# k_m and v_m as plain f32 products with the k and v tiles stationary

## The chip, the core and the metric

The kernel runs on one core of a Trainium2 chip. A core has TensorE (PE, matrix products; PEld is its weight load), VectorE (DVE), ScalarE (ACT) and GpSimd (POOL), and DMA queues, of which SyncE's (SP) carries most loads here. A matrix product takes a *stationary* operand, loaded as weights, and streams a *moving* operand past it; results go to one of eight PSUM banks. The metric is the device time of one execution in microseconds (us); the median of three runs before the change is 1393.74 us.

## The reference

Eight batches, eight heads, 576 rows of length 64, 32 memory slots; then a dense mixture of four experts over all 4608 rows.

```python
a = exp(phi - phi.max(axis=2)); a = a / (a.sum(axis=2) + 1e-9)     # over the 576 rows
k_m = einsum('bhsm,bhsd->bhmd', a, k)
v_m = einsum('bhsm,bhsd->bhmd', a, v)
scores = (q @ k_m^T) / 8
attn = exp(scores - scores.max(-1)); attn = attn / (attn.sum(-1) + 1e-9)
x = (attn @ v_m) laid out as 4608 x 512
p = domain_probs / (domain_probs.sum(-1) + 1e-9)
out = sum over e of p[:, e] * (relu(x @ w1[e]) @ w2[e])             # 512 -> 1024 -> 512
```

All arrays are f32, and the result has to be good to more digits than one rounded product gives.

## The kernel before

**Precision.** TensorE takes f32 in two ways here. The big products run on `float32r` tiles, a rounded form. Where more digits are needed a tile is split in two float32r parts: ACT casts it (the high part) and POOL or DVE subtracts the cast from the original (the low part). A product of split operands is three float32r products (high·high, high·low, low·high). Transposes (a product with the identity `ident`) and `scores_mm` (q·k_m) run on plain f32 tiles, not split.

**Stages.** Batches are worked in four pairs; each pair is 128 *steps* (`PAIR`), four experts of 32. Attention never forms `attn @ v_m`: the kernel multiplies v_m by w1 (`vw_mm`, `vw_out`, tiles `vw`, or `four_*` and DRAM for later experts), and a step's `first(s)` multiplies that by the transposed softmax `AT` (L641 to L643), applies relu (ACT L653, DVE L655) to make `h`, and `second(s)` multiplies `h` by `w2` (L674 to L676) into an accumulating bank. The last two pairs use another scheme with fewer products (`unit`, L916 to L918 and L1002).

**k_m and v_m, the part that changes.** For each batch `phi` is exponentiated and normalized (`phi_max`, `phi_exp`, `phi_norm`), turned by transposes (`phi_turn`, `phi_turn_tail`) and split into tile `a` (L308/L309, L323/L324): 128 rows of s by (high, low) by two heads by 32 slots. k and v of a head pair `hp` come as one 512 KB load, `kv`, four chunks of 128 rows with k beside v, into one of four `stage` buffers; `kv_split` casts and subtracts it (L345, L346) into `kvs`. `kv_mm` (L357) then takes `a` (high and low side by side, 128 columns) as weights and streams the 256 columns of k and v: for each chunk one product with the high part of kv and one with the low part. The last 64 rows come as `kvt`, loaded twice over so that high and low sit on different halves of the partitions (`tail_split`, L331/L332), and are one product (`kv_mm_tail`, L360). The sum has slots in rows; `kv_out` copies it (L368), `kv_fold` transposes it back (L377, `ident`), and `kv_pick` copies the high half and adds the low half into `kT` and `v` (L394, L396).

**Order.** `at(s, unit)` puts units in a plan by step; the tables `UNITS_1`, `ATT` and so on set them by hand. From step 36 on, and in the start-up before step 0, instructions stand in the order of the program; for steps 0 to 35 a scheduler orders them. Batch 0's k_m and v_m are made in the start-up, batch 1's in the scheduled steps, batches 2 to 7 at hand-set steps beside the expert products. Loads into `stage` are issued in plan order, three takes ahead (`take`, `stage_ahead`). The four banks "pm" are shared by `first`, `vw_mm`, the transposes and the k_m/v_m sums in rotation. `keep_warm` issues idle products of `ident`.

**Softmax over slots.** `soft` sums each row's 32 exponentials (L490), adds 1e-9 (L491), takes the reciprocal (L492) and multiplies (L493).

Of the kernel before, what the change touches and what calls it, by code (L numbers as in the profile page):

```python
# [61 lines left out]
UNITS_1 = (1, 5, 5, 6, 5, 6, 8, 9, 10, 11, 11, 12, 17, 13, 13, 20)  # L62
# [21 lines left out]
def body(ctx: ExitStack, tc: tile.TileContext, qm, qt, kv, kvt, phi, prob, w1, w1d, w2, out):  # L84
# [41 lines left out]
    def stage_ahead(upto):  # L126
        while count[0] < min(upto, len(order)):
# [16 lines left out]
            )  # L144
            nc.sync.dma_start(t, src)
# [131 lines left out]
    def phi_norm(b, g):  # L277
# [27 lines left out]
    def phi_turn_out(b, g):  # L305
        src = st["tpa", b, g].rearrange("p c a m -> p a c m")
        dst = st["a", b][:, 2 * g:2 * g + 2, :4]
        nc.scalar.copy(dst[:, :, :, 0, :], src)  # L308
        nc.vector.tensor_sub(dst[:, :, :, 1, :], src, dst[:, :, :, 0, :].bitcast(F32))  # L309
        give(st["tpa", b, g])  # L310

    def phi_turn_tail(b):
        ph = st["ph", b]
        tp = bank("pm", NP, 2 * M)
        for g in range(2):
            nc.tensor.transpose(
                tp[:, 2 * g:2 * g + 2].rearrange("p a m -> p (a m)"), ph[:, g, 512:], ident
# [3 lines left out]
    def phi_turn_tail_out(b):  # L321
        a, tp = st["a", b], st["tpb", b]
        nc.scalar.copy(a[:, :, 4, 0, :], tp)  # L323
        nc.vector.tensor_sub(a[:, :, 4, 1, :], tp, a[:, :, 4, 0, :].bitcast(F32))  # L324
# [9 lines left out]
    def unit_tail(b):
        def emit(raw):
            for h in range(2):
                tail_split(b, raw, h, nc.gpsimd)
        return ("kvt", b), emit

    def kv_split(b, hp, raw, c2, eng):  # L340
        tag = {"tag": "kvs", "bufs": KVS} if b else {"tag": "vw1", "bufs": 5}
        t = att.tile([P, 2, 512], F32R, name="kvs", **tag)
        t = t.rearrange("p s (i d) -> p s i d", i=2)
        src = raw[:, 2 * c2:2 * c2 + 2].rearrange("p c w d -> p c (w d)")
        nc.scalar.copy(t[:, 0], src)  # L345
        eng.tensor_sub(t[:, 1], src, t[:, 0].bitcast(F32))  # L346
        st["kvs", b, hp, c2] = t

    def kv_mm(b, hp, c2):
        if c2 == 0:  # L350
            st["x", b, hp] = bank("pm", 2 * P)
        x, a, t = st["x", b, hp], st["a", b], st["kvs", b, hp, c2]
        for i in range(2):
            c = 2 * c2 + i
            lhs = a[:, hp, c].rearrange("p s m -> p (s m)")
            for s in range(2):
                nc.tensor.matmul(x, lhs, t[:, s, i, :], start=c + s == 0, stop=False)  # L357

    def kv_mm_tail(b, hp):
        nc.tensor.matmul(  # L360
            st["x", b, hp],
            st["a", b][:, hp, 4].rearrange("p s m -> p (s m)"), st["tail", b][:, hp, :],
            start=False, stop=True,
        )

    def kv_out(b, hp):
        xs = att.tile([P, 2 * P], F32, name="xs", tag="xs", bufs=2)
        nc.scalar.copy(xs, st["x", b, hp])  # L368
        give(st["x", b, hp])
        st["xs", b, hp] = xs  # L370
# [903 lines left out]
```

## Time and profile before

| | |
|---|---|
| median of 3 runs | 1393.74 us (1391.53 to 1394.98) |
| profiled execution | 1392.14 us, span of its instructions 1390.3 us |
| TensorE busy | 1362.0 us, 98% of the span |
| DVE, ACT, POOL busy | 841.3, 625.4, 617.4 us (61%, 45%, 44%) |
| granted TensorE clock, mean | 0.997 |
| DMA | 301.37 MB, 217 GB/s |

A row of the profile names the line, engine and operation, the tiles written and read, the shape and the count. "128\*128 128x256" on a PE row is the weights (rows\*columns) and then the output. Durations of PE rows overlap, since products are pipelined: what a product costs in a stream is the distance from its start to the next start, which I take from merged timeline rows (first column start, second length, both us; "x8" is eight records merged).

### The profile page before, as it was taken

The page shows a single profiled execution, that of the slowest core. Times are in us where ns is not written, and L with a number is a line of the kernel's source. Part 1 is how long each engine was busy: PE and PEld are TensorE (multiplying, and loading weights), DVE is VectorE, ACT ScalarE, POOL GpSimd, SP SyncE. Part 2 cuts the span into 40 slices and gives each one's busy share as a digit, 9 for nine tenths or more (in the row PEclk, how much of TensorE's full clock was granted, in tenths as well). Part 3 has the DMA queues.
Part 4 walks back from the last instruction along what each step waited for, and adds up shares of the span by engine and source line. Part 5 has one row for each costly group of instructions (what it writes and reads, how often), then busy time and mean ns, then how long its engine had stood idle before and what let it go on. Part 6 is the DMA issues. An engine that isn't in the chain of part 4 may idle for free.

```text
span 1390.3 us, 25223 instructions
## 1 busy us (share of the span) xinstructions
PE 1362.0 (98%) x8894; PEld 1248.4 (90%) x8894; DVE 841.3 (61%) x1894; ACT 625.4 (45%) x1536; POOL 617.4 (44%) x652
## 2 busy tenths in 40 slices
PE   7999999999999999999999999999999999999998
PEld 6788888788888888889888998999999999999998
DVE  7875535446755365454434467777767666666666
ACT  6765555443345465463344354555543333333332
POOL 4400354745353424433144375677753334443432
PEclk9999999999999999999999999999999999999999
DMA  6742354897675364354598898899984866666661
GB/s 255 240 165 76 117 182 173 311 322 240 210 281 212 107 229 146 125 203 143 178 290 296 277 321 292 286 344 311 326 298 131 259 186 177 180 173 175 175 181 75
DMA packets 102029, 301.37 MB, mean 217 GB/s; under 512 B 24976, under 2 KB 26128, under 8 KB 101904
## 3 DMA queue, kind: packets, MB, share of 16 engines
q1 hardware_dynamic: 81168, 224.26, 51.9%
q0 software_dynamic: 19584, 71.31, 13.0%
q10 hardware_dynamic: 1152, 4.19, 0.7%
q8 instruction: 71, 1.16, 0.3%
q14 instruction: 54, 0.44, 0.1%
HBM read 213.46 MB, written 84.93 MB: 215 GB/s over the span
## 4 chain that ended last, share of the span: by engine, by line
PE 89%; DVE 4%; DMA 2%; issue 2%; ACT 1%; SPq 0%; POOL 0%; DVEq 0%; ACTq 0%; POOLq 0%
PE banks L1002 22%; PE banks L676 9%; PE banks L674 9%; PE banks L675 9%; PE banks L916 5%; PE banks L917 5%; PE banks L918 5%; PE banks L641 5%; PE banks L642 4%; PE banks L643 4%; PE banks L579 3%; PE banks L463 2%; PE banks L357 2%; DMA stage<-in_w 1%; PE banks L1040 1%
## 5 line engine op out<-in xcount | busy, mean ns | idle before, releaser
L1020 DVE SCALAR_TENSOR_TENSOR acc<-banks,pt,acc 128x256 f32<-128x256 f32 x416 | 200.0, 481 | 107.7 <-PE banks L1002 104.2
L160 POOL TENSOR_TENSOR w<-stage,w 128x512 fp32r<-128x512 f32 x134 | 177.0, 1332 | 188.7 <-ACT w L159 179.4
L655 DVE SCALAR_TENSOR_TENSOR h<-banks,h 128x256 fp32r<-128x256 f32 x256 | 107.3, 420 | 168.6 <-ACT h L653 111.4
L676 PE MATMUL banks<-w,h 128*128 128x512 f32 x512 | 201.2, 393 | 3.4 <-DVE h L655 3.4
L674 PE MATMUL banks<-w,h 128*128 128x512 f32 x512 | 201.9, 394 | 0.1
L675 PE MATMUL banks<-w,h 128*128 128x512 f32 x512 | 201.4, 393 | 0.0
L653 ACT ACTIVATE h<-banks 128x256 fp32r<-128x256 f32 x256 | 98.0, 384 | 199.8 <-PE banks L643 169.9
L641 PE MATMUL banks<-AT,vw 128*128 128x256 f32 (+1 forms) x512 | 156.6, 306 | 3.7 <-DVE h L655 1.8
L1002 PE MATMUL banks<-w,a 128*128 128x256 f32 x1080 | 154.4, 282 | 0.3 <-DVE acc L1020 0.2
L643 PE MATMUL banks<-AT,vw 128*128 128x256 f32 (+1 forms) x512 | 150.9, 295 | 1.2 <-DVE vw L556 1.2
L916 PE MATMUL banks<-AT,vw 128*128 128x256 f32 (+1 forms) x512 | 151.6, 296 | 0.0
L642 PE MATMUL banks<-AT,vw 128*128 128x256 f32 (+1 forms) x512 | 151.3, 296 | 0.0
L917 PE MATMUL banks<-AT,vw 128*128 128x256 f32 (+1 forms) x512 | 151.1, 295 | 0.0
L918 PE MATMUL banks<-AT,vw 128*128 128x256 f32 (+1 forms) x512 | 150.9, 295 | 0.0
L1002 PEld LDWEIGHTS banks<-w,a 128*128 128x128 f32 x1080 | 143.6, 188 | 4.8 <-issue 0.9
L983 POOL TENSOR_TENSOR vt<-ph,vt 128x512 fp32r<-128x512 f32 x64 | 84.1, 1314 | 107.3 <-ACT vt L982 78.3
L676 PEld LDWEIGHTS banks<-w,h 128*128 128x128 f32 x512 | 96.3, 188 | 25.8 <-DVE h L655 4.3
L346 POOL TENSOR_TENSOR kvs<-stage,kvs 128x512 fp32r<-128x512 f32 x58 | 75.4, 1317 | 93.2 <-ACT kvs L345 87.3
L641 PEld LDWEIGHTS banks<-AT,vw 128*128 128x128 f32 x512 | 96.8, 189 | 13.8 <-DVE vw L556 3.8
L674 PEld LDWEIGHTS banks<-w,h 128*128 128x128 f32 x512 | 96.4, 188 | 12.0 <-ACT h L653 0.4
L675 PEld LDWEIGHTS banks<-w,h 128*128 128x128 f32 x512 | 96.4, 188 | 10.9
L159 ACT CAST w<-stage 128x512 fp32r<-128x512 f32 x168 | 102.7, 619 | 4.5 <-DMA stage<-in_w 2.1
(149 smaller groups left out, 2985.4 us busy)
## 6 DMA issues: line engine op xcount, KB each, us to landing
w<-kw SPq DMA_DIRECT2D x93, 512.0 KB, 5.5
vwd<-vst POOLq DMA_DIRECT2D x80, 512.0 KB, 6.4
vw<-vwd SPq DMA_DIRECT2D x320, 128.0 KB, 6.0
w<-v SPq DMA_DIRECT2D x55, 512.0 KB, 5.6
stage<-in_w SPq DMA_DIRECT2D x44, 512.0 KB, 4.5
stage<-in_w1d SPq DMA_DIRECT2D x40, 512.0 KB, 5.3
stage<-in_kv SPq DMA_DIRECT2D x32, 512.0 KB, 4.3
kw<-w POOLq DMA_DIRECT2D x24, 512.0 KB, 5.6
```

Source lines behind the costliest of these rows:

```text
L160: eng.tensor_sub(dst[:, 1, :], raw, dst[:, 0, :].bitcast(F32))
L641: nc.tensor.matmul(ps, w[:, 0, f], at_t[:, g, 0, c], start=g == 0, stop=False)
L642: nc.tensor.matmul(ps, w[:, 0, f], at_t[:, g, 1, c], start=False, stop=False)
L643: nc.tensor.matmul(ps, w[:, 1, f], at_t[:, g, 0, c], start=False, stop=g == 1)
L674: nc.tensor.matmul(po[t], x[:, 0, :], w[:, 0, :], start=j == 0, stop=False)
L675: nc.tensor.matmul(po[t], x[:, 0, :], w[:, 1, :], start=False, stop=False)
L676: nc.tensor.matmul(po[t], x[:, 1, :], w[:, 0, :], start=False, stop=j == NJ - 1)
L916: nc.tensor.matmul(ps, w[:, 0, f], at_t[:, g, 0, c], start=g == 0, stop=False)
L917: nc.tensor.matmul(ps, w[:, 0, f], at_t[:, g, 1, c], start=False, stop=False)
L918: nc.tensor.matmul(ps, w[:, 1, f], at_t[:, g, 0, c], start=False, stop=g == 1)
L1002: nc.tensor.matmul(ps, a[:, l, jj], w[:, r, c], start=start and jj + i == 0, stop=jj == 1 and i == 2, skip_group_check=True,)
L1020: VE.scalar_tensor_tensor(a, src, p, a, ALU.mult, ALU.add)
```

## The change

Five things:

1. `a` and the tail `tl` become plain f32, not split; `kv_split`, `tail_split`, `kv_out`, `kv_fold` are gone. `kv_mm` takes the raw `stage` tile as weights (128 rows by the 128 columns of k or v of a head pair) and streams `a` of that pair (64 columns), so that the result has the 64 entries of k or v in rows, as `kT` and `v` want it. Per batch: 4 pairs, k and v, 4 chunks and a tail, that is 40 products.
2. All of a batch's sums lie in one bank (`kvp`), picked by four copies.
3. `kvt` is loaded once over (64 rows, 256 KB), straight into `tl` by `load_tail`, outside the `stage` rotation.
4. The start-up's order is rewritten; for batch 0 the low half of `vt` is subtracted by POOL, not by DVE.
5. In `soft` the addition of 1e-9 becomes a sum over a pair whose second element is 1e-9 from a memset.

The hand-set steps: batches 2 to 7 multiply at s+13, s+14, s+15, s+16 (one pair a step) and pick at s+17; before, they multiplied at s+12, s+15, s+18, s+21. The tail's step in `UNITS_1` goes from 5 to 2.

```diff
     def phi_turn_out(b, g):
         src = st["tpa", b, g].rearrange("p c a m -> p a c m")
-        dst = st["a", b][:, 2 * g:2 * g + 2, :4]
-        nc.scalar.copy(dst[:, :, :, 0, :], src)
-        nc.vector.tensor_sub(dst[:, :, :, 1, :], src, dst[:, :, :, 0, :].bitcast(F32))
+        (nc.vector.tensor_copy if b == 0 and g else nc.scalar.copy)(
+            st["a", b][:, 2 * g:2 * g + 2, :4], src
+        )
...
+    def load_tail(b):
+        st["tail", b] = att.tile([P, NP, 2 * P], F32, name="tl", tag="tl")
+        nc.sync.dma_start(st["tail", b][:64], kvt[b])
+
+    def kv_mm(b, hp, raw):
+        if hp == 0:
+            st["kvp", b] = bank("pm", 2, NP, 2 * M)
         for w in range(2):
+            x = st["kvp", b][:, w, hp]
+            for c in range(4):
+                nc.tensor.matmul(x, raw[:, c, w], st["a", b][:, hp, c], start=c == 0, stop=False)
+            nc.tensor.matmul(
+                x, st["tail", b][:64, hp, P * w:P * w + P], st["a", b][:64, hp, 4],
+                start=False, stop=True,
             )
...
     def soft(b, t0):
...
-        nc.vector.reduce_sum(zv[:, :, 0], av, AX.X)
-        nc.vector.tensor_scalar_add(zv[:, :, 0], zv[:, :, 0], 1e-9)
+        sums_z = guarded.popleft()
+        guarded.append(sums_z)
+        nc.vector.reduce_sum(sums_z[:n, :nt * H, 0], av, AX.X)
+        nc.vector.reduce_sum(zv[:, :, 0], sums_z[:n, :nt * H], AX.X)
...
-        at(s + 9, unit_tail(b))
+        at(s + 6, lambda: load_tail(b))
         for hp in range(NP):
...
-            at(s + 10 + 3 * hp, (("kv", b, hp), load))
-            at(s + 12 + 3 * hp, multiply)
-            at(s + 13 + 3 * hp, lambda hp=hp: kv_out(b, hp))
-        for g in range(2):
-            at(s + 18 + 6 * g, lambda g=g: [kv_fold(b, 2 * g + i) for i in range(2)])
-            at(s + 19 + 6 * g, lambda g=g: kv_pick(b, g))
+            at(s + 13 + hp, (("kv", b, hp), lambda raw, hp=hp: kv_mm(b, hp, raw)))
+        at(s + 13 + NP, lambda: kv_pick(b))
```

The new line numbers: `kv_mm` L339 and L340 (tail), transposes L303 and L319, `scores_mm` L415, `vw_mm` L489 to L491, `first` L595 to L597, `second` L628 to L630, `keep_warm` L1060, splits L163/L164.

On PE, in the start-up, where batch 0's sums end and the first scores begin (`kvs`, `tl`, `a` as above, `xs` the copied sum, `w` a split w1 tile, `vt` the split v_m). Before:

```order
L360 MATMUL banks<-tl,a 128x256
L377 MATMUL banks<-ident,xs 128x128 x4
L357 MATMUL banks<-kvs,a 128x256 x8
L360 MATMUL banks<-tl,a 128x256
L1118 MATMUL banks<-ident 128x128 x3
L463 MATMUL banks<-kT_78,stage 128x64 x4
L377 MATMUL banks<-ident,xs 128x128 x4
L1118 MATMUL banks<-ident 128x128 x5
L463 MATMUL banks<-kT_78,stage 128x64 x4
L1118 MATMUL banks<-ident 128x128 x2
L535 MATMUL banks<-w_255,vt_82 128x512
```

After:

```order
L339 MATMUL banks<-a,stage 128x64 x4
L340 MATMUL banks<-a,stage 128x64
L415 MATMUL banks<-kT_78,stage 128x64 x8
L1060 MATMUL banks<-ident 128x128 x4
L489 MATMUL banks<-w_242,vt_82 128x512
```

The transposes between the halves of the scores are gone; the scores follow the last sum directly.

On POOL, in the start-up, behind the memsets. Before:

```order
L115 MEMSET vt_83 128x1024
L346 TENSOR_TENSOR kvs<-stage,kvs 128x512
L332 TENSOR_TENSOR tl<-stage,tl 64x512
L346 TENSOR_TENSOR kvs<-stage,kvs 128x512
L332 TENSOR_TENSOR tl<-stage,tl 64x512
L160 TENSOR_TENSOR w_255<-stage,w_255 128x512
```

After:

```order
L115 MEMSET vt_83 128x1024
L118 MEMSET zg_90 128x16
L118 MEMSET zg_91 128x16
L378 TENSOR_TENSOR vt_82<-v,vt_82 64x2x32 x4
L164 TENSOR_TENSOR w_242<-stage,w_242 128x512
L164 TENSOR_TENSOR w_245<-stage,w_245 128x512
L164 TENSOR_TENSOR vh<-v,vh 128x128
```

POOL's splits of k, v and the tail are gone; four subtractions for `vt` now stand ahead of the w1 splits.

On PE, for batch 2, one head pair at its step. Before:

```order
L676 MATMUL banks<-w_1375,h 128x512
L357 MATMUL banks<-kvs,a 128x256 x8
L360 MATMUL banks<-tl,a 128x256
L377 MATMUL banks<-ident,xs 128x128 x4
L641 MATMUL banks<-AT,vw 128x320
```

After:

```order
L630 MATMUL banks<-w_1112,h 128x512
L339 MATMUL banks<-a,stage 128x64 x4
L340 MATMUL banks<-a,tl 128x64
L339 MATMUL banks<-a,stage 128x64 x4
L340 MATMUL banks<-a,tl 128x64
L595 MATMUL banks<-AT,vw 128x256
```

Nine products of 256 columns and their transposes become ten products of 64 columns, read from the loaded `stage` tile itself.

More of the change, by code (lines that the diff above doesn't have):

```diff
@@ L60 @@
 }
[L62 removed]
+UNITS_1 = (1, 5, 5, 6, 2, 6, 8, 9, 10, 11, 11, 12, 17, 13, 13, 20)
 W1_1 = (10, 10, 12, 13)
@@ L115, in body @@
         nc.gpsimd.memset(t, 0.0)
+    guarded = deque(const.tile([P, 2 * H, 2], F32, name=f"zg{i}") for i in range(2))
+    for t in guarded:
+        nc.gpsimd.memset(t[:, :, 1], 1e-9)
     pt = const.tile([P, N // P, E], F32, name="pt")
@@ L144, in stage_ahead @@
             )
+            t = t[:src.shape[0]]
             nc.sync.dma_start(t, src)
@@ L334, in unit_tail @@
[L334 to L370, printed above, removed]
-    def kv_fold(b, hp):
-        g = hp // 2
-        if hp % 2 == 0:
-            st["kvp", b, g] = bank("pm", 2, 2, P)
-        for w in range(2):
-            nc.tensor.transpose(
-                st["kvp", b, g][:, hp % 2, w, :], st["xs", b, hp][:, w * P:(w + 1) * P], ident
-            )
-    def kv_pick(b, g):
-        if g == 0:
+    def load_tail(b):
+        st["tail", b] = att.tile([P, NP, 2 * P], F32, name="tl", tag="tl")
+        nc.sync.dma_start(st["tail", b][:64], kvt[b])
@@ L387, in kv_pick @@
                 r, m = slice(64 * i, 64 * i + 64), slice(M * i, M * i + M)
[L388 to L397 removed]
+                dst = st["v", b][r, hps] if w else kT[b % 4][r, hps, m]
+                (nc.vector.tensor_copy if b == 0 and i else nc.scalar.copy)(
+                    dst, st["kvp", b][r, w, hps, m]
+                )
+        if hps.stop == NP:
+            give(st["kvp", b])
     def unit_kv(b, hp):
         def emit(raw):
[L401 to L410 removed]
+            kv_mm(b, hp, raw)
+            if hp == NP - 1:
+                kv_pick(b)
         return ("kv", b, hp), emit
@@ L1150, in body @@
-        kv_split(0, 3, kvr(3), 0, dve)
+        st["tail", 0] = raw["kvt", 0]
+        q = raw["qm", 0, 0]
         for hp in range(2):
-            for c2 in range(2):
-                kv_mm(0, hp, c2)
-            kv_mm_tail(0, hp)
-        kv_split(0, 3, kvr(3), 1, dve)
-        for hp in range(2):
-            kv_out(0, hp)
-        for hp in (2, 3):
-            for c2 in range(2):
-                kv_mm(0, hp, c2)
-            kv_mm_tail(0, hp)
-            if hp == 2:
-                for i in range(2):
-                    kv_fold(0, i)
@@ L1177, in body @@
-        kv_pick(0, 1)
+        kv_pick(0, slice(2, 4))
         scores_mm(0, 0, q, (2, 3))
         scores_max(0, 0)
-        split_w1(w1g[0], 0, 1, gps)
-        write_vt_0(0, slice(1, 2))
-        keep_warm(2)
-        split_w1(w1g[1], 0, 2, gps)
-        split_w1(w1g[1], 0, 3, gps)
-        pv = [vw_mm(0, 0, hp, ("p2", 4)) for hp in range(4)]
+        write_vt_0(0, gps)
+        keep_warm(4)
+        w1g = [raw["w1", 0, 0, g] for g in range(2)]
+        for hp in range(2):
+            split_w1(w1g[0], 0, hp, gps)
@@ L1186, in body @@
         scores_exp(0, 0)
-        vw_out(pv[0], 0, 0, 0, 0, (0,))
+        pv = [vw_mm(0, 0, hp, ("p2", 4)) for hp in range(2)]
+        for hp in range(2, 4):
+            split_w1(w1g[1], 0, hp, gps)
+        pv += [vw_mm(0, 0, hp, ("p2", 4)) for hp in range(2, 4)]
         soft(0, 0)
-        keep_warm(3)
-        for hp in (1, 2):
+        for hp in (0, 1):
             vw_out(pv[hp], 0, 0, 0, hp, (0,))
@@ L1194, in body @@
         transposes_out(0, 0)
-        vw_out(pv[3], 0, 0, 0, 3, (0,))
+        for hp in (2, 3):
+            vw_out(pv[hp], 0, 0, 0, hp, (0,))
         for i in range(2):
```

86 lines of the change are left out of this document (18 added, 68 removed).

## The prediction

> **What bounds the kernel now.** I read the busy times first, then TensorE's share by stretches, then its rows by shape and the distances between them, then its waits, last the start-up in order of time. The page and the stretches (length, then busy time and records of each engine, granted clock, DMA share, GB/s):
>
> ```profile
> PE 1362.0 (98%) x8894; PEld 1248.4 (90%) x8894; DVE 841.3 (61%) x1894; ACT 625.4 (45%) x1536; POOL 617.4 (44%) x652
> ...
> 0.00:40.00 40.00, 28.52 (x177) 24.98 (x178) 31.21 (x65) 26.15 (x61) 17.86 (x23) 0.96 0.69 252
> 40.00:60.00 20.00, 18.62 (x113) 15.73 (x112) 17.75 (x39) 16.03 (x35) 7.21 (x6) 1.00 0.69 234
> 60.00:780.00 720.00, 710.85 (x4006) 620.49 (x4005) 377.52 (x852) 339.82 (x888) 282.58 (x273) 1.00 0.60 203
> ```
>
> From 60 us on PE has a product in flight nearly always, and the other engines about half the time. There the time is the sum of PE's distances; work taken from DVE, ACT and POOL is worth only the PE waits that it causes. Before 60 us PE is idle 11.5 + 1.4 us, and DVE is the busiest. So the change has two prices: PE's own products (everywhere), and the start-up.
>
> **PE's price of k_m and v_m.** First the rows by shape (busy, mean ns):
>
> ```profile
> L357 PE MATMUL banks<-kvs,a 128*128 128x256 f32 x256 | 36.3, 284 | 2.8 <-DVE a L309 1.9 <-DVE kvs L346 0.9
> L463 PE MATMUL banks<-kT,stage 128*128 128x64 f32 x256 | 30.8, 272 | 0.8 <-DVE kT L396 0.7
> L377 PE MATMUL banks<-ident,xs 128*128 128x128 f32 x64 | 10.0, 273 | 0.0
> L360 PE MATMUL banks<-tl,a 128*128 128x256 f32 x32 | 9.1, 284 | 0.4 <-DVE a L324 0.4
> L463 PE MATMUL banks<-kT,stage 128*64 128x64 f32 x64 | 5.4, 228 | 0.3 <-DVE AT L526 0.3
> ```
>
> L463, q·k_m, is the nearest row to a new product: plain f32 on both sides, 128 rows, 128 columns of weights, 64 columns streamed. The count tells the main thing. The program has 8 batches of two 256-row groups with 8 such products, 128 in all; the profile has 256 records. L357 has 256 products and 256 records, L377 64 and 64. So a plain f32 product runs as two records, each with its own weight load, a float32r one as one. What a record takes is read from distances:
>
> ```profile
> 523.29 0.39 PE L676 MATMUL banks<-w,h 128*128 128x512 f32 x1
> 523.52 1.89 PE L463 MATMUL banks<-kT,stage 128*128 128x64 f32 x16
> 525.22 0.36 PE L641 MATMUL banks<-AT,vw 128*128 128x256 f32 x1
> ...
> 590.71 1.11 PE L357 MATMUL banks<-kvs,a 128*128 128x256 f32 x8
> 591.65 0.28 PE L360 MATMUL banks<-tl,a 128*128 128x256 f32 x1
> 591.77 0.60 PE L377 MATMUL banks<-ident,xs 128*128 128x128 f32 x4
> 592.12 0.36 PE L641 MATMUL banks<-AT,vw 128*128 128x256 f32 x1
> ...
> 38.29 0.68 PE L463 MATMUL banks<-kT,stage 128*64 128x64 f32 x8
> 38.90 0.50 PE L535 MATMUL banks<-w,vt 128*128 128x512 f32 x1
> ```
>
> - Old product: (591.65 - 590.71)/8 = 0.1175 us. Old fold: (592.12 - 591.77)/4 = 0.0875 us.
> - New product: (525.22 - 523.52)/16 = 0.106 us a record, 0.2125 us a product. With weights 64 columns wide the record takes (38.90 - 38.29)/8 = 0.076: the width of the weights matters though the stream is 64 columns both times. The new weights are 128 wide.
>
> A batch gave up 32 + 4 products and 8 folds, 36 x 0.1175 + 8 x 0.0875 = 4.93 us, and gets 40 x 0.2125 = 8.50. Net +3.57 us a batch. Batches 1 to 7 lie in the PE-bound stretch: **+25.0 us**. The tail's 8 products a batch have 64 rows of weights, which no plain f32 row shows. From below they are bounded by the 0.076 of the narrow row (112 records x 0.030 = 3.4 us less), from above by 0.106; I take 0.106, because the narrow row differs in columns, which the tail does not. The Trainium skill, "TensorE: Matmul & The Clock Gate", section LDWEIGHTS, says that a weight load takes its columns over 1.2 in ns whatever the rows, 107 ns for 128; by that the tail's price is the one taken, and no price here falls below it. The 128-wide rows agree (0.106 a record); for 64 columns it would be 53 ns and the trace has 76. The transposes of phi's tail get narrower weights (2 a batch): 14 x at most 0.03, nothing.
>
> **What the other engines give back.** Their splits go (POOL's L346 and L332, ACT's L345, L331, L368, DVE's L309, L324, L396). After 60 us only PE's waits count; the longest of them:
>
> ```profile
> PE banks L579 <- ACT h L653: 2.5, 1, 2.5
> PE banks L676 <- DVE h L655: 2.0, 1, 2.0
> PE banks L1002 <- DVE acc L1020: 1.9, 4, 1.2
> PE banks L641 <- DVE h L655: 1.8, 1, 1.8
> PE banks L641 <- DVE vw L556: 1.7, 3, 0.9
> ```
>
> The second is the pair sum's business. DVE and POOL at that place:
>
> ```profile
> 333.73 0.68 DVE L490 TENSOR_REDUCE z<-at 128x16 f32<-128x512 f32 x1
> 334.10 5.49 POOL L160 TENSOR_TENSOR w<-stage,w 128x512 fp32r<-128x512 f32 x4
> 334.44 5.19 DVE L491 TENSOR_SCALAR z<-z 128x16 f32<-128x16 f32 x1
> ...
> 339.67 0.25 DVE L492 RECIPROCAL z<-z 128x16 f32<-128x16 f32 x1
> ```
>
> Adding 1e-9 to 16 numbers took 5.19 us, until POOL's run of four subtractions ended; the sum beside it (L490) was not held. The `h` that stood behind it on DVE came late, and PE waited 2.0 us. The new sum is of L490's kind, so I count these 2.0 us as gained. Of the others, L579 waits behind `vst`'s transfers and L1002 behind the accumulation, neither touched; of the two L641 rows (3.5 us) ACT's lighter load may give back a little, 0 to 2. I take 2.5 in all, bounds 0 and 5.
>
> **The start-up.** Which instructions carry it now:
>
> ```profile
> 7.12 1.14 ACT L345 CAST kvs<-stage 128x512 fp32r<-128x512 f32 x2 [0.82 <-DMA stage<-in_kv]
> 7.98 0.38 PE L316 MATMUL banks<-ident,ph 128*128 128x128 f32 x2
> ...
> 20.91 1.10 PE L463 MATMUL banks<-kT,stage 128*128 128x64 f32 x8 [0.68 <-DVE kT L396]
> 26.24 0.39 PE L537 MATMUL banks<-w,vt 128*128 128x512 f32 x1
> 30.06 1.11 PE L514 MATMUL banks<-ident,at 128*128 128x128 f32 x4 [2.76 <-DVE at L493]
> 32.53 0.77 PE L641 MATMUL banks<-AT,vw 128*128 128x256 f32 x2
> 37.17 0.50 PE L676 MATMUL banks<-w,h 128*128 128x512 f32 x1 [1.37 <-DVE h L655]
> ...
> 17.79 1.27 POOL L160 TENSOR_TENSOR w<-stage,w 128x512 fp32r<-128x512 f32 x1 [3.52 <-ACT w L159]
> 28.39 0.46 POOL L160 TENSOR_TENSOR vh<-v,vh 128x128 fp32r<-128x128 f32 x1 [3.06 <-ACT vh L159]
> 32.42 1.66 ACT L159 CAST w<-stage 128x512 fp32r<-128x512 f32 x3
> ```
>
> The new chain: kv's first load is there at 7.1, the turns end near 8.4. 40 products take 8.5 us (to 16.9), 8 score products 1.7: the last score stands at 18.6, before at 20.91 + 0.9. The softmax is then ready about 4 us later (max, subtract, exp, sum and product, each of 512 elements a row as L490 above, 0.68, and two small ones). But PE's next work, the 12 v·w1 products, waits for POOL, and that chain is the later one: v is picked at 17.3, four `vt` subtractions of at most 0.46 end by 19.1, four w1 splits of 1.27 with `vh` 0.46 among them by 24.7. The last product ends at 25.4 (before 26.5), and the transposes, behind it on PE, start there, not at 30.06. From the transposes to the first `first` it is 2.5 us (30.06 to 32.53), through the same cast and subtraction: 27.9. From there to L676 it is 4.6 us, 1.4 of them PE's wait for an `h` that DVE made late behind splits; ACT still has casts ahead of the first relu (four, where the row above has three in 1.66), so I leave 3.2 us. The first complete `second` is at about 31, where L676 now starts at 37.17: **-6 us**, bounds -2 (POOL's chain stretched, and the 1.4 kept) and -9 (transposes bound by the softmax alone). From there to 60 us DVE is nearly full; it loses L309, L324 and POOL's company, worth at most the 1.4 us of PE idle in that stretch: -1. What `kvt`'s half load saves ahead of the products is within these bounds.
>
> **New waits.** PE now reads `stage` itself, so a late kv load stops PE, with all that is queued on it; before, it stopped ACT two steps ahead. One place is tight. The third kv load of batch 3 now stands behind the sixteen small copies of batch 2's v on SP's queue; the first and the last of them:
>
> ```profile
> 193.90 0.60 SPq L448 DMA_DIRECT2D vs<-vh  x1
> 206.69 0.61 SPq L450 DMA_DIRECT2D vt<-vh  x1
> ```
>
> They hold the queue 13.4 us. The product that needs the load comes three steps after the copies are due; a step is six products at 0.1175 and six at 0.23 (523.29 to 523.52), 2.1 us, and one with kv work 4.2, so about 10.5 us pass. 0 to 4 us may be lost; I take 0.5. `load_tail` is three steps ahead of its use on the same queue, and `tl` is free by then. One bank of "pm" is held five steps on end; three remain for `first`, which needs a bank again only three steps later: nothing.
>
> **The sum.** 25.0 - 2.5 - 6 - 1 + 0.5 = +16.0 us. The profiled execution took 1392.14 (span 1390.3), so 1408.1; the median of the runs is 1.6 above it, so **1409.5**.
>
> **Rivals.**
>
> 1. *A product costs what its 256 streamed columns cost in float32r (faster).* Then 280 products x 0.1175 = 32.9 against 34.5 given up, -1.6, and with -9.0 for the rest 1383. Against it stand the two records of every L463 product. It decides below (34.5 + 9.0 - 4.2)/280 = 0.140 us a product; 0.2125 was measured. The Trainium skill, "FP8 and Floating Point Precision", section TensorE Precision Notes, gives true f32 four passes through the array; four passes of 64 columns would be this rival, and the two records speak against that reading. Chance 0.03.
> 2. *The records run at the narrow row's pace (no change).* 560 x 0.076 = 42.6, +8.1, less 9.0: 1393. Against it: the 16 records in a row of L463 with just the new shape. Chance 0.05.
> 3. *PE starves for kv.* Each of batches 2 to 7 waits once for a load or a bank, 1 to 2 us, and batch 3 the full 4: +8 to +14 on top, 1418 to 1424. For it: the queue row above; against it: loads are three takes ahead, 11 us or more. Chance 0.12.
>
> My forecast has 0.80. A measurement of this kernel can tell about 0.3%, 4.2 us, from no change. Faster by more: 0.03 and a little, 0.04; within: 0.05; slower: 0.91. The forecast's own bounds: 25.0 less 3.4, gains of 12 to 4 in the start-up and the waits together, new waits 0 to 4: 1403 to 1418. For 8 in 10 I widen it to 1401 and, towards the third rival, 1420.
>
> **What the profile after would show.** L339 with 512 records and L340 with 128, sixteen of a kind at 0.106 us from start to start; else the PE term falls. The span from 60 us on longer by about 3.6 us for each batch, in the stretches where the kv products stand, and nowhere else. The first L630 near 31 us; the 1e-9 sum never above 0.3 us; the 2.0 us wait of `second` gone. A PE wait on `stage` at L339, above all in batch 3, would be the third rival.

## Result, and the profile after

The changed kernel takes 1434.89 us (median of 6 runs, 1433.82 to 1441.27) against 1394.11: 1.0306 times as long, 95% interval 1.0284 to 1.0328. The forecast was 1409.5 us, with a range of 1401 to 1420. The sign was right; the loss is 41 us instead of 16. The profiled execution has a span of 1432.8 us, 42.5 more than before's.

The page, busy times and the granted clock in 40 slices:

```profile
PE 1412.0 (99%) x9164; PEld 1290.2 (90%) x9164; DVE 799.0 (56%) x1793; ACT 566.8 (40%) x1375; POOL 524.7 (37%) x584
...
PEclk7999999999999999999999999999999999999999
```

The other engines lost work as the diff says, PE's share rose, and the first slice has a clock of 0.7 where before had no slice below 0.9. The new products by shape (busy, mean ns | idle before):

```profile
L339 PE MATMUL banks<-a,stage 128*128 128x64 f32 x512 | 71.3, 285 | 1.3 <-DVE v L352 1.1 <-DMA stage<-in_kv 0.2
L340 PE MATMUL banks<-a,tl 64*128 64x64 f32 x112 | 24.2, 296 | 0.0
```

With the 16 records of batch 0's tail that is 512 and 128, two for each plain f32 product, as forecast. What they take is read from the starts. One head pair of a later batch in the kernel after, where PE is never idle:

```profile
685.02 1.00 PE L339 MATMUL banks<-a,stage 128*128 128x64 f32 x8
685.95 0.43 PE L340 MATMUL banks<-a,tl 64*128 64x64 f32 x2
686.31 1.10 PE L339 MATMUL banks<-a,stage 128*128 128x64 f32 x8
687.35 0.43 PE L340 MATMUL banks<-a,tl 64*128 64x64 f32 x2
687.71 0.41 PE L595 MATMUL banks<-AT,vw 128*128 128x320 f32 x1
```

20 records take 687.71 - 685.02 = 2.69 us, 0.134 each; the forecast had 0.106. Two tail records alone take 0.36.

The start-up in order of time, and by stretches (length, busy time and records of PE, PEld, DVE, ACT, POOL, granted clock, DMA share, GB/s):

```profile
8.57 1.08 PE L339 MATMUL banks<-a,stage 128*128 128x64 f32 x8 [0.20 <-DMA stage<-in_kv]
...
13.84 0.43 PE L340 MATMUL banks<-a,stage 64*128 64x64 f32 x2
...
15.38 1.97 PE L339 MATMUL banks<-a,stage 128*128 128x64 f32 x8 [1.11 <-DVE v L352]
...
42.37 0.73 PE L630 MATMUL banks<-w,h 128*128 128x512 f32 x2 [0.79 <-DVE h L609]
```
```profile
8.00:15.00 7.00, 6.04 (x44) 5.15 (x41) 0.92 (x2) 1.04 (x4) 0.00 (x0) 0.96 1.02 386
15.00:25.00 10.00, 9.62 (x39) 8.79 (x40) 0.23 (x1) 0.07 (x1) 0.00 (x0) 0.50 0.86 309
```

From 15 to 25 us PE is busy 9.62 of 10 us at half its clock, and a group of eight records takes 1.97 us instead of 1.08. The granted clock changes to one half at 14.4 us and returns at 31.5. PE's wait of 1.11 us begins only at 14.27 (15.38 - 1.11). The first complete `second` stands at 42.37; before it was 37.17, forecast was 31.

How far the kernels stand behind before at the same `second`, from the starts of its third product in each trace (us; the number is the record's index, of 576 in all):

| kernel | 0 | 24 | 60 | 128 | 200 | 300 | 400 | 511 | end |
|---|---|---|---|---|---|---|---|---|---|
| before, at | 37.2 | 84.1 | 126.8 | 216.7 | 310.3 | 435.1 | 567.8 | 704.9 | 1390.3 |
| after | +5.2 | +11.2 | +11.3 | +26.2 | +21.8 | +21.9 | +33.4 | +43.8 | +42.5 |
| e4, new start-up alone | +4.4 | +4.8 | +4.9 | +5.3 | +3.8 | +3.9 | +3.8 | +3.9 | +2.0 |
| e6, tails of 128 rows | +0.5 | +4.2 | +4.3 | +14.2 | +9.8 | +10.7 | +17.8 | +23.7 | +21.6 |
| e5, mended start-up alone | -5.8 | -5.1 | -3.3 | -2.6 | -5.9 | -5.2 | -5.3 | -5.2 | -7.0 |
| e8, whole change, mended | -6.4 | -1.5 | -1.4 | +8.3 | +6.1 | +7.6 | +14.7 | +20.8 | +19.3 |

After loses 5 us at the start and about 5.8 with each batch's k_m and v_m, and nothing in the second half of the program, where no batch is made. It gains 4.4 us once, between 217 and 310. Of these 1.4 are order alone: at 217 before still has work of batch 3 ahead (its last fold stands at 232.6), while after has done it. The other 3.0 come in one place: in the profiled execution of before PE idled 3.1 of the 10 us from 268 on, at a mean clock of 0.83; in after it idled 1.25 at full clock (first before, then after):

```profile
268.00:278.00 10.00, 6.88 (x27) 5.51 (x27) 3.66 (x9) 4.49 (x12) 5.42 (x6) 0.83 0.79 274
```
```profile
293.00:303.00 10.00, 8.75 (x42) 6.80 (x42) 3.85 (x10) 4.79 (x14) 5.74 (x7) 1.00 0.87 282
```

### The profile page after: what moved, and what is told of

Read it like the earlier page. It is cut to its first block, busy times and chain, and to the rows that moved or that the text cites. A ratio compares the mean times of both kernels' runs of the same rounds, so it can differ in the third digit from the quotient of the medians.

```text
span 1432.8 us, 25323 instructions
## 1 busy us (share of the span) xinstructions
PE 1412.0 (99%) x9164; PEld 1290.2 (90%) x9164; DVE 799.0 (56%) x1793; ACT 566.8 (40%) x1375; POOL 524.7 (37%) x584
## 4 chain that ended last, share of the span: by engine, by line
PE 91%; DVE 4%; issue 2%; DMA 1%; ACT 1%; POOL 1%; SPq 0%; DVEq 0%; ACTq 0%; POOLq 0%
PE banks L944 22%; PE banks L628 9%; PE banks L629 9%; PE banks L630 8%; PE banks L595 5%; PE banks L858 5%; PE banks L859 5%; PE banks L860 5%; PE banks L339 5%; PE banks L597 4%; PE banks L596 4%; PE banks L533 2%; PE banks L415 2%; PE banks L340 2%; PE banks L982 1%
## 5 line engine op out<-in xcount | busy, mean ns | idle before, releaser
L164 POOL TENSOR_TENSOR w<-stage,w 128x512 fp32r<-128x512 f32 x134 | 178.3, 1345 | 362.7 <-ACT w L163 291.3
L630 PE MATMUL banks<-w,h 128*128 128x512 f32 x512 | 201.1, 393 | 2.7 <-DVE h L609 2.7
L628 PE MATMUL banks<-w,h 128*128 128x512 f32 x512 | 202.3, 395 | 0.0
L595 PE MATMUL banks<-AT,vw 128*128 128x256 f32 (+1 forms) x512 | 158.2, 309 | 3.5 <-DVE vw L510 2.2
L597 PE MATMUL banks<-AT,vw 128*128 128x256 f32 (+1 forms) x512 | 151.0, 296 | 1.8 <-DVE vw L510 1.8
L630 PEld LDWEIGHTS banks<-w,h 128*128 128x128 f32 x512 | 96.2, 188 | 25.3 <-DVE h L609 3.6
L595 PEld LDWEIGHTS banks<-AT,vw 128*128 128x128 f32 x512 | 96.3, 188 | 15.3 <-DVE vw L510 2.9
L944 PE MATMUL banks<-w,y 128*128 128x256 f32 x732 | 108.2, 281 | 0.0
L628 PEld LDWEIGHTS banks<-w,h 128*128 128x128 f32 x512 | 96.4, 188 | 12.2 <-issue 0.2
L163 ACT CAST w<-stage 128x512 fp32r<-128x512 f32 x168 | 102.4, 618 | 10.0 <-DMA stage<-in_w 6.7
L596 PEld LDWEIGHTS banks<-AT,vw 128*128 128x128 f32 x512 | 97.1, 190 | 8.3 <-DVE AT L480 0.4
L944 PEld LDWEIGHTS banks<-w,y 128*128 128x128 f32 x732 | 98.8, 188 | 1.8 <-DVE acc L962 0.2
```

The lines of the kernel that those rows point to most:

```text
L164: eng.tensor_sub(dst[:, 1, :], raw, dst[:, 0, :].bitcast(F32))
L595: nc.tensor.matmul(ps, w[:, 0, f], at_t[:, g, 0, c], start=g == 0, stop=False)
L596: nc.tensor.matmul(ps, w[:, 0, f], at_t[:, g, 1, c], start=False, stop=False)
L597: nc.tensor.matmul(ps, w[:, 1, f], at_t[:, g, 0, c], start=False, stop=g == 1)
L628: nc.tensor.matmul(po[t], x[:, 0, :], w[:, 0, :], start=j == 0, stop=False)
L630: nc.tensor.matmul(po[t], x[:, 1, :], w[:, 0, :], start=False, stop=j == NJ - 1)
```

## Experiments

Two things had to be explained: records of 0.134 us, and a start-up at half clock with a busy PE. My theory: (a) each change of the weights' row count, 128 to 64 or back, costs 0.14 us; (b) the clock follows how much of the array streams, not whether PE has a product in flight. Rivals: a 64-row record is slow by itself; the clock fell because of PE's 1.1 us wait at 15.4.

**e1: the pair sum alone.** Before, with the guard tile and the second sum (one tile instead of two).

```diff
-nc.vector.reduce_sum(zv[:, :, 0], av, AX.X)
-nc.vector.tensor_scalar_add(zv[:, :, 0], zv[:, :, 0], 1e-9)
+nc.vector.reduce_sum(sums_z[:n, :nt * H, 0], av, AX.X)
+nc.vector.reduce_sum(zv[:, :, 0], sums_z[:n, :nt * H], AX.X)
```

> The kernel before with the pair sum alone (one guard tile instead of two). Theory (the hold only moves on): the 5.2 us hold at 334 us leaves the 1e-9 step, which takes 0.19 us, and falls on the next DVE instruction that stands beside POOL's run of four subtractions (the reciprocal or the 512-element product); the 2.0 us wait of `second` behind `h` stays. 1394 us, within 1 of before. Rival (as predicted): the hold goes with the instruction, PE's 2.0 us wait goes, 1392.

Measured: 1395.96 us, 1.0015 times before in the same session (95% interval 1.0005 to 1.0026; the later runs are given in the same way). The order of time at the place in e1:

```profile
338.79 0.19 DVE L496 TENSOR_REDUCE z<-zg 128x16 f32<-128x32 f32 x1
338.90 5.52 POOL L163 TENSOR_TENSOR w<-stage,w 128x512 fp32r<-128x512 f32 x4
339.01 0.25 DVE L497 RECIPROCAL z<-z 128x16 f32<-128x16 f32 x1
339.30 5.68 DVE L498 TENSOR_TENSOR at<-at,z 128x512 f32<-128x512 f32 x1
...
345.97 0.80 PE L681 MATMUL banks<-w,h 128*128 128x512 f32 x1 [2.01 <-DVE h L660]
```

The 1e-9 step is down to 0.19 us, and the hold of over 5 us sits two instructions further on, in the product by the reciprocal (0.69 us elsewhere). PE waits 2.01 us as before. The same stands in the kernel after:

```profile
356.22 0.19 DVE L445 TENSOR_REDUCE z<-zg 128x16 f32<-128x32 f32 x1
356.31 5.54 POOL L164 TENSOR_TENSOR w<-stage,w 128x512 fp32r<-128x512 f32 x4
...
356.73 5.68 DVE L447 TENSOR_TENSOR at<-at,z 128x512 f32<-128x512 f32 x1
```

So the theory of a hold that moves on stands, and the pair sum is worth nothing there. It even came out 2 us slower, where 1394, within 1 of before, was expected. In its profile, which is of its slowest run (1400.47), the clock is at half for six periods of 3.4 us before 705 us, where before has two. Each of the five falls stands at a PE wait of 1.8 to 3.1 us: the wait of 2.01 us above ends at 345.97, and the clock falls at 345.9. Before waits about as long at the same place (2.03 us, up to 341.6) and keeps its clock there, so such a wait can bring a fall and need not; what decides is not shown.

**e2: the tails of a batch together.** After, with all eight tail products ahead of the 32 others.

```diff
+for i in range(2 * NP):               # with hp == 0: all tails of the batch
+    w, t = i % 2, i // 2
+    nc.tensor.matmul(st["kvp", b][:, w, t], tail[:64, t, P * w:P * w + P], a[:64, t, 4], start=True, ...)
...
-    nc.tensor.matmul(x, tail[:64, hp, P * w:P * w + P], a[:64, hp, 4], start=False, stop=True)
```

> The kernel after with the eight 64-row tail products of a batch in one run ahead of the 32 products of 128 rows, so that the weights' row count changes twice a batch instead of sixteen times; the number of records is the same. Theory (each change of row count costs 0.14 us): a batch's products take 8.5 + 0.3 = 8.8 us instead of 10.35, seven batches give -11, 1424 us. Rival 1 (a record with 64 rows is slow by itself, 0.18 us instead of 0.11): no change, 1435. Rival 2 (no 64-row surcharge, the time lies in the switch between rows of any weights): no change, 1435.

Part of the tails' sums is lost in this kernel; number, shape and order of the products are as said. Measured: 1428.46, 1.0246 (1.0228 to 1.0264), 6.4 below after, and 6.6 in the span, where 11 was expected. The products themselves came out as the theory has them. The first head pair of batch 2, with all tails ahead:

```profile
161.84 2.00 PE L338 MATMUL banks<-a,tl 64*128 64x64 f32 x16
163.76 2.00 PE L345 MATMUL banks<-a,stage 128*128 128x64 f32 x16
165.57 0.52 PE L600 MATMUL banks<-AT,vw 128*128 128x256 f32 x1
```

It takes 165.57 - 161.84 = 3.73 us, and the three others 1.70 each (169.31 to 171.01), so a batch takes 8.83 us, where after takes 4 x 2.69 = 10.76 and 8.8 was expected. Seven batches are 13.5 us less. About half of that goes to the clock: after the start-up e2's profile has five periods of 3.4 us at half clock, after's has one, and e2's five begin 3.5 to 3.9 us after the start of a run of tails (here at 165.6); two of the seven runs bring none. At half clock a PE that is always busy loses 1.7 us a period, so four more of them are an estimated 6.8 us. Tails that stand together thus save the changes of row count and bring falls of the clock instead. e3 measures the pieces.

**e3: bursts.** Before, with extra products out of `ident` and `vts[0]` into a free bank, every 26 steps.

```diff
+for kind in range(7):
+    at(70 + 26 * kind, lambda kind=kind: burst(kind))
```

> The kernel before with seven bursts of extra products, 26 steps apart, in the stretch where PE never idles; outputs unchanged. (0) 150 plain f32 products 128x128 by 64 columns, (1) the same with 128 columns, (2) 150 float32r products 128x128 by 64 columns, (3) 64 plain f32 products by 64 columns with the weights' rows alternating 128 and 64, (4) 64 of them all with 64 rows, (5) 20 times five plain f32 products by 64 columns and one float32r product by 512, (6) the same with two by 512. Theory A (the clock falls where PE streams few columns, however busy): in burst 0 the granted clock falls to 0.5 within 7 us and the records go from 0.11 to 0.21 us, 33 us becomes about 58; in burst 1 (as many records, twice the columns) it stays at 1.0, 33 us; burst 2 tells whether float32r falls as well. Rival B (the clock fell behind the 1.1 us wait of the start-up): no burst falls, since none has a wait within. Row changes: burst 3 takes 14 us + 64 x 0.14 = 23 us at full clock if a change costs 0.14, burst 4 14 us; if a 64-row record is slow by itself, burst 4 takes 23 us. Total 1390 + about 180 us at full clock, 205 to 220 with falls.

A stretch inside each burst, 0 to 6 in this order (columns as above):

```profile
258.00:278.00 20.00, 20.00 (x181) 20.00 (x181) 0.00 (x0) 0.00 (x0) 0.00 (x0) 1.00 0.14 39
365.00:385.00 20.00, 20.00 (x182) 20.00 (x181) 0.00 (x0) 0.00 (x0) 0.00 (x0) 1.00 0.34 134
472.00:490.00 18.00, 18.00 (x86) 18.00 (x86) 0.00 (x0) 0.00 (x0) 0.00 (x0) 0.50 0.21 87
572.00:592.00 20.00, 20.00 (x66) 16.14 (x66) 0.00 (x0) 0.00 (x0) 0.00 (x0) 0.50 0.00 1
688.00:701.00 13.00, 13.00 (x63) 13.00 (x63) 0.00 (x0) 0.00 (x0) 0.00 (x0) 0.50 0.00 0
785.00:805.00 20.00, 20.00 (x166) 19.36 (x165) 0.00 (x0) 0.00 (x0) 0.00 (x0) 1.00 0.00 1
885.00:905.00 20.00, 20.00 (x155) 18.93 (x153) 0.00 (x0) 0.00 (x0) 0.00 (x0) 1.00 0.62 174
```

The span grew by 212.6 us. PE is busy in all of the stretches throughout. Theory A missed on burst 0: plain f32 with 128 rows and 64 columns holds the full clock for its 33 us. Rival B missed on three others: without any wait they halved the clock after 4 to 5 us, float32r with 128 rows and 64 columns (2), plain f32 with rows alternating (3), plain f32 with 64 rows (4). The mixtures with products of 512 columns (5 and 6) hold it. So no wait is needed, and "few columns" alone is not the measure; rows and the kind of product count too.

Row changes: at full clock the records of burst 4 start 0.112 us apart, as those of burst 0, so 64 rows cost nothing by themselves. In burst 3 before the clock fell they start 0.205, 0.160, 0.202 and 0.160 apart, 0.727 for four records and two changes, where four of one kind take 0.447: **0.14 us a change**. The weight loads show where it goes: in burst 0 a load starts 0.056 us after the start of the product before it, and 0.056 us ahead of its own product; in burst 3 the first load of another row count starts 0.204 us after that product's start, together with its own product.

**e4: the new start-up alone.** Before, with batch 0 by the changed path and the changed order, batches 1 to 7 and the 1e-9 as before.

```diff
-kv_split(0, 0, kvr(0), 0, gps) ... kv_mm(0, hp, c2) ... kv_fold(0, i) ... kv_pick(0, 0)
+phi_turn_n ... kv_mm_n(0, hp, kvr(hp)) ... kv_pick_n(0, slice(0, 2)) ... (as in the kernel after)
```

> The kernel before with the changed path for batch 0 alone (the changed start-up: plain f32 products, no splits, reordered); batches 1 to 7 split and fold as before, and 1e-9 is added as before. Theory (start-up and steady products are two separate losses): the granted clock halves near 14 us as in the kernel after, the first complete `second` stands at 42 us instead of 37, 1394 + 5 = 1399. Rival (the start-up loss comes from work of batch 1 that the change also altered): 1388 to 1394, first complete `second` near 31 to 37.

Measured: 1395.1, 1.0017 (1.0004 to 1.003), less than the 1399 expected. The clock halves as in after, the first complete `second` stands at 41.54, and the table has +4.9 us at record 60. The end is only 2 us behind, since 3.4 of it come back, near 272 us (1.5) and behind 705 (1.9). The start-up and the later products are two separate losses.

**e5 and e5b: a start-up that fills the array.** e4, with batch 0's tail taken as 128 rows (rows 64 to 127 of `a` are zeros, those of the tail's tile its second copy), a bank for each half of k_m and v_m, and the first two w1 splits ahead of the scores. e5b is the same with 64 rows in the tail.

```diff
+gps.memset(st["a", 0][64:, :, 4], 0.0)                              # e5 only
-x, st["tail", b][:64, hp, P * w:P * w + P], st["a", b][:64, hp, 4]
+x, st["tail", b][:, hp, P * w:P * w + P], st["a", b][:, hp, 4]      # e5 only
-if hp == 0: st["kvp", b] = bank("pm", 2, NP, 2 * M)
+if hp % 2 == 0: st["kvp", b, hp // 2] = bank("pm", 2, 2, 2 * M)
+split_w1(w1g[0], 0, 0, gps); split_w1(w1g[0], 0, 1, dve)            # ahead of the scores
```

> The kernel before with a changed start-up alone, as in e4, but batch 0's tail padded with zero rows to 128 (no product with 64 rows), each half of k_m and v_m in a bank of its own (so PE has no wait in mid-way), and the first two w1 splits issued ahead of the scores. Theory (the clock fell at the start-up because products with 64 columns and 64 rows fill too little of the array, and products of 128 rows by 64 columns hold a full clock, as burst 0 did, but can't raise a halved one): the clock stays at 1.0 through the kv products, which take 9 us and end near 17.5, the first complete `second` is at 29 to 32 us instead of 37.2 (before) and 41.5 (e4), total 1386 to 1389. Rival (any plain f32 product with 64 columns lets the clock fall in the start-up, whatever its rows): clock 0.5 from 11 to 15 us on, first `second` near 39, total 1392 to 1395.

> As e5, with the one difference that the tail's products have 64 rows again. Theory (rows decide): the clock halves within 7 us of the first product although PE has no wait, first complete `second` 4 to 8 us later than in e5. Rival (the 1.1 us wait was the cause): the clock stays, and e5b differs from e5 by the eight changes of row count alone, 2.2 us.

Measured: e5 1387.68, 0.9958 (0.9943 to 0.9973), faster than before; e5b 1395.9, 1.0019 (1.0009 to 1.0028). Stretches of e5, then its first complete `second` in order of time; behind them the same two of e5b:

```profile
8.00:15.00 7.00, 7.00 (x64) 6.98 (x63) 1.15 (x3) 2.01 (x6) 0.14 (x1) 1.00 1.03 418
15.00:25.00 10.00, 9.12 (x66) 7.92 (x66) 6.63 (x11) 5.78 (x15) 5.39 (x8) 1.00 0.85 318
```
```profile
31.41 0.73 PE L731 MATMUL banks<-w,h 128*128 128x512 f32 x2 [0.78 <-DVE h L710]
```
```profile
8.00:15.00 7.00, 6.99 (x49) 6.29 (x47) 1.13 (x3) 0.97 (x5) 0.00 (x0) 0.93 1.02 415
15.00:25.00 10.00, 10.00 (x42) 9.06 (x41) 1.80 (x3) 1.96 (x6) 1.40 (x2) 0.50 0.82 298
```
```profile
39.84 0.73 PE L731 MATMUL banks<-w,h 128*128 128x512 f32 x2 [0.78 <-DVE h L710]
```

Eight products with 64 rows among forty make the difference of 8.4 us at this place; 2.2 of it are their sixteen changes of row count at 0.14, the rest is the clock. PE is busy 7.00 and 6.99 of the first 7 us, so no wait halves e5b's clock (at 14.0 us). e5b is what decides between the theory and its rival.

**e6: tails of 128 rows in every batch.** After, padded as in e5, with its start-up otherwise unchanged.

```diff
+nc.gpsimd.memset(st["a", b][64:, :, 4], 0.0)
-nc.sync.dma_start(st["tail", b][:64], kvt[b])
+nc.sync.dma_start(st["tail", b], kvt[b])
```

> The kernel after with every batch's tail padded by zero rows to 128: the same 640 records, none with 64 rows. Theory: a batch's products take 20 records a head pair at 0.112 less the first, 8.75 us instead of 10.35; seven batches give -11 us; the start-up still has its 1.1 us wait, so the clock falls there at most later; 1435 - 11 - (0 to 8) = 1416 to 1424. Rival (the surcharge of the tail products has another cause than their row count): 1435.

Measured: 1414.02, 1.0153 (1.0127 to 1.0179), 21 below after, a little more than the 11 to 19 expected. One head pair in e6:

```profile
666.60 1.00 PE L340 MATMUL banks<-a,stage 128*128 128x64 f32 x8
667.44 0.39 PE L341 MATMUL banks<-a,tl 128*128 128x64 f32 x2
667.66 1.06 PE L340 MATMUL banks<-a,stage 128*128 128x64 f32 x8
668.55 0.39 PE L341 MATMUL banks<-a,tl 128*128 128x64 f32 x2
668.75 0.40 PE L596 MATMUL banks<-AT,vw 128*128 128x320 f32 x1
```

As many records take 2.15 us; the 0.54 that is saved is four changes of 0.135. Its start-up keeps the 1.1 us wait, and its clock falls too, at 16.6 us for 10.2 us, where after's fell at 14.4 for 17.1. With full rows and no wait (e5) it doesn't fall. On PE the wait is what differs between the two up to there, so beside the rows the wait seems to count as well; no run changes it alone.

**e7: more bursts.** Same place as e3, other products (`hm` is the real data of burst 1).

> The kernel before with six bursts in the stretch where PE never idles; outputs unchanged. (0) 70 float32r products 128x128 by 64 columns, then 150 plain f32 ones by 64 columns; (1) 150 plain f32 products by 64 columns on real data instead of an identity; (2) 15 times four plain f32 products with 128 rows and one with 64, as in the kernel after; (3) 64 float32r products by 256 columns with rows alternating 128 and 64; (4) 64 plain f32 products with 64 rows by 128 columns; (5) 150 float32r products by 128 columns. Theory (the clock goes by the share of the array that streams, with different bounds for falling and rising): the clock falls in the first part of (0) and does not rise in its second; (1) holds 1.0; (2) falls within 7 us, or, if 37% is above the bound, holds; (4) and (5) hold, since each has twice the columns of a burst that fell. Rival on the data (the identity's zeros mattered in burst 0): (1) falls. Row changes: if they cost 0.14 us with float32r too, (3) takes 64 x 0.117 + 64 x 0.14 = 16 us, else 7.5.

Stretches in the second part of burst 0, then in bursts 1 to 5:

```profile
260.00:325.00 65.00, 65.00 (x306) 65.00 (x306) 0.00 (x0) 0.00 (x0) 0.00 (x0) 0.50 0.02 9
405.00:430.00 25.00, 25.00 (x227) 25.00 (x225) 0.00 (x0) 0.00 (x0) 1.33 (x2) 1.00 0.43 151
515.00:538.00 23.00, 23.00 (x94) 20.88 (x93) 0.00 (x0) 0.00 (x0) 0.00 (x0) 0.50 0.16 65
618.00:640.00 22.00, 22.00 (x44) 12.30 (x43) 0.00 (x0) 0.00 (x0) 0.00 (x0) 0.50 0.00 0
724.00:736.00 12.00, 12.00 (x109) 12.00 (x109) 1.07 (x5) 2.12 (x6) 1.26 (x1) 1.00 0.10 40
816.00:830.00 14.00, 14.00 (x127) 14.00 (x127) 0.00 (x0) 0.00 (x0) 0.00 (x0) 1.00 0.06 22
```

In burst 0 the float32r products let the clock fall at 254.2, 3.6 us after their start, and the plain f32 products that held the full clock in e3's burst 0 leave the halved one at 0.50 for 64 us (first row). They start 0.213 us apart there, not 0.112, so they stream half as much per us; whether the clock rises at another bound than it falls is not shown. Real data changes nothing (second row). With the mixture of the kernel after, four products of 128 rows to one of 64, the clock falls 6.3 us after the start (third). With twice the columns, the 64-row products and the float32r ones hold the clock (last two). The fourth row is float32r by 256 columns with alternating rows, where the clock falls too: ahead of the fall its records start 0.31 us apart, 0.19 more than the 0.1175 of a row of equal ones, so float32r pays for the change as well.

**e8: the whole change, mended.** e6 with e5's start-up.

> The whole change with both causes taken out: every tail padded by zero rows to 128 as in e6, and the start-up of e5 (a bank for each half, two w1 splits ahead of the scores). If the two causes are all that the forecast missed, the clock holds from the first raise on, the first complete `second` stands at 31 to 32 us, a batch's products take 8.65 us as in e6, and the total is e6's 1414 less the 5 to 6 us that the start-up differs: 1407 to 1410, as forecast for the change. If something else had made up the miss, it ends at 1412 or more.

Measured: 1409.89 (1408.8 to 1411.43), 1.0115 (1.0097 to 1.0132). The first complete `second`, at full clock up to there:

```profile
30.78 0.73 PE L630 MATMUL banks<-w,h 128*128 128x512 f32 x2 [0.50 <-DVE h L609]
```

With both causes out, the change costs about what was forecast, in part by luck (see the sum below).

**e9, e10, e11: what holds DVE.** All are e5 with some of POOL's subtractions given to DVE: e9 every second split of the doubled w1 parts, e10 expert 0's w1 splits in `units_w1`, e11 expert 3's w2 splits.

```diff
 # e11, in units_w2
-split_w2(k, e, 2 * j2, raw, nc.gpsimd)
+split_w2(k, e, 2 * j2, raw, nc.vector if e == 3 else nc.gpsimd)      # and the same for 2 * j2 + 1
```

> As e5 (the fastest so far, 1387.7), with every second split of the doubled w1 parts done by DVE instead of POOL, so that POOL's run of four subtractions at 330 us becomes two. Theory (DVE's long instruction there lasts because of POOL's run): no DVE instruction there above 3.3 us, PE's 2.0 us wait of `second` gone or below 0.5 us; 1385 to 1388, since DVE takes 16 x 0.69 us of work more. Rival (the hold has another cause): the 5 us hold and the 2.0 us wait stay, 1388.

> As e5, with the eight splits of expert 0's next w1 parts (the ones that form POOL's run of four at 331 us) done by DVE instead of POOL, so that nothing of that run is left on POOL there. Theory (a DVE instruction that reads two operands, or the 1e-9 step, has to wait while POOL subtracts): no DVE instruction near 331 us above 2 us, PE's 2.0 us wait of `second` gone or below 0.7 us; the time 1385.5 to 1388, as DVE has 5.5 us of work more in that stretch. Rival (the hold has another cause): the 5 us hold and the 2.0 us wait stay.

> As e5, with the eight w2 splits of expert 3 on DVE instead of POOL (the run of four at 329 us is made of these: it stands behind the two stores of `v` and ahead of the next `raw` subtractions on POOL's queue). Theory (the 5 us hold is a DVE instruction that waits while POOL subtracts): no DVE instruction above 2 us there and PE's 2.0 us wait of `second` below 0.7 us; 1385.5 to 1388, with eight times 0.69 us more on DVE. Rival (the hold has another cause): an instruction of about 5 us and the 2.0 us wait stay.

Measured: e9 1400.13, 1.0058 (1.0039 to 1.0077); e10 1387.82, 0.9956 (0.9941 to 0.9971); e11 1384.7, 0.993 (0.9911 to 0.9949). The edits of e9 and e10 missed the run: it, the hold and the wait stood as in e5, and e9's extra work on DVE showed as new waits (5.7 us at L1057 instead of 1.9). In e10 the 1e-9 step still takes 5.20 us beside four subtractions. e11 took the run away. The same step twice in e11, the first beside a run of two other subtractions on POOL, the second where before had the run of four:

```profile
321.74 2.74 POOL L214 TENSOR_TENSOR raw<-raw,sv 128x512 fp32r<-128x512 f32 x2
321.76 2.77 DVE L546 TENSOR_SCALAR z<-z 128x16 f32<-128x16 f32 x1
...
332.85 0.17 DVE L546 TENSOR_SCALAR z<-z 128x16 f32<-128x16 f32 x1
```

Beside four POOL subtractions the step takes 5.2 us, beside two 2.77, beside none 0.17, and PE's 2.0 us wait is gone. So POOL's run is the cause. e11 has the lowest median of this study; its interval and that of e5 overlap slightly.

## Why the prediction was wrong, by its steps

- *Bound by PE; other engines' work is worth only PE's waits.* Right. POOL lost 93 us and DVE 42 of busy time, and the kernel is slower by PE's products and the start-up.
- *Two records for a product.* Right: 512 and 128. Rival 1 (one price of 0.1175 a product) is out, as is rival 2: a record of 128 rows is 0.108 on average (e6: 2.15/20), just above the 0.106 of the forecast.
- *The tail's price, "I take 0.106".* This is the first step that failed. The tail was bounded from above by the row of a run of equal records, and the change from one row count to another got no price. The prediction says that no plain f32 row has weights of 64 rows. That is a misreading: before has 16 such records, the transposes of the softmax's last 64 rows, and they show a change as well.

```profile
L514 PE MATMUL banks<-ident,at 64*128 64x64 f32 x16 | 2.7, 247 | 0.0
...
108.60 0.39 PE L676 MATMUL banks<-w,hm 128*128 128x512 f32 x1
108.92 0.33 PE L514 MATMUL banks<-ident,at 64*128 64x64 f32 x2
109.18 0.42 PE L641 MATMUL banks<-AT,vw 128*128 128x320 f32 x1
```

The first 64-row record starts 0.32 us after the start of one of 512 columns, where otherwise 0.23 pass (523.29 to 523.52). So the trace of before gave a sign of the cost. A record of 64 rows costs the same as one of 128 in a run of its own (burst 4), and the change costs 0.14, 16 times a batch. A batch takes 4 x 2.69 = 10.8 us, not 8.50; seven batches +41 instead of +25.0. In e6 it is 4 x 2.15 = 8.6, +26. The sentence from the Trainium skill, "TensorE: Matmul & The Clock Gate", section LDWEIGHTS (rows don't matter to a weight load), agrees with burst 4. It does not speak of a change between row counts; it made me put no price on one, and took away the upper side of the bound.
- *The start-up, -6.* The second step that failed, worth 11 us after the 16 of the products: it took each duration at full clock, and the new products let the clock fall. 42.37 us instead of 31, so +5.2. With tails of 128 rows and no wait (e5, e8) the first complete `second` stands at 31.41 and 30.78; the chain of v, `vt` and w1 that the forecast followed was read rightly. The Trainium skill, "TensorE: Matmul & The Clock Gate", section "Part 1: The HAM clock gate", ties the clock to how busy PE has been. The rows of e5b (6.99 of 7 and 10.00 of 10 us busy, and a clock that falls to 0.50) show that a busy PE in the profile's sense is not enough.
- *-2.0 for the pair sum's hold.* Failed: the hold went to another instruction (5.68 us in after and in e1), and PE's wait stayed at 1.96. The price was put on the instruction that was held instead of on the run beside it (e11). The Trainium skill, "SBUF — State Buffer", section "SBUF: two separate sides", gives DVE and GpSimd a common port pair under a lock, for which a DVE instruction in a two-port mode or with two SBUF inputs has to wait until a GpSimd instruction that started first is done. The rows agree as far as they go: in e1 the second sum and the reciprocal, with one input each, took 0.19 and 0.25 us beside the run's start, the product by the reciprocal, with two, 5.68. They show the hold last through a run of four subtractions, not through one. By that page of the Trainium skill the hold would have moved to the product, and this term of the forecast would have been 0.
- *-1 for the stretch from 40 to 60 us.* Not seen: from record 0 to record 24 after loses 6.0 us, as much as batch 1's products alone (5.8).
- *+0.5 for kv loads, rival 3.* After shows PE waiting on `stage` for 0.2 us in all, at 8.57. Not seen. A single bank held for a whole batch cost nothing later, and 1.1 us in the start-up.
- *The sum.* 16 forecast; 41 - 25 = 16 from the products and 5.2 + 6 = 11 from the start-up make 43, the measured span +42.5. The other terms are small: 2.0 and 1 that didn't come, 4.4 that came between 217 and 310 us. (As written, 1408.1 + 1.6 makes 1409.7, not 1409.5.)

e8 comes to 1409.9 against the forecast 1409.5. The two large terms are as forecast: -6.4 at the first `second` (forecast -6), and 8.6 us a batch (8.50). That the sum meets so closely is luck: the 2.0 of the hold are not gained in e8 either (PE waits 1.94 us there), and its profiled execution, the slowest of its four runs, ends 19.3 us behind before's, not 16.

## What to carry to other kernels

A price read from a run of equal instructions doesn't hold where the new code alternates two shapes: count the changes of shape as well as the instructions. Look through all rows for one with such a change, also one of another line, and where there is none, take the upper bound as open. Before a chain is re-timed with other products, ask whether they fill the array as well as the old ones, since durations at full clock hold only as long as the clock does. An instruction that is held by something beside it is not the cause: removing it hands the hold to the next of its kind, removing the run beside it ends it (e11).

## What the runs showed of the hardware

- A change between weights of 128 and of 64 rows costs 0.14 us with plain f32 and 0.19 with float32r by 256 columns, and the next weight load starts late (0.204 and 0.31 us after the start of the product before it); rows of zeros in `a` that keep the count at 128 save it on PE (2.15 us instead of 2.69 for 20 records) for a tail load of twice the size.
- The granted clock falls with PE busy throughout. Held: plain f32 128 rows by 64 columns, plain f32 64 by 128, float32r 128 by 128. Fell: plain f32 64 by 64, float32r 128 by 64, four of the first kind with one of 64 by 64, and both kinds of alternating rows. An estimate that orders all of these bursts is rows times columns per us, counted twice in a plain f32 record: 146,000 (2 x 128 x 64 in 0.112 us) held; the mixture (ten records, 147,456 in 1.40 us, or 105,000) and all below it fell. No burst lies between the two.
- The clock of a burst that fell did not rise by itself: at half clock the products that held a full one did not bring it back in 64 us; in the start-up of after it came back once 128-column and 512-column products followed.
- The stretches at half clock that end inside the program are whole multiples of 3.41 us long: 3.41 in most runs, 10.24 in e6, 17.07 in after, 27.31 and 37.55 in e3.
